# Cosine operands of an attention and expert kernel: the second batch scaled once, other ticks, own buffers for the first

## The chip, the cores and the metric

The kernel runs on one core of a Trainium2 chip. The metric is device time in microseconds (us), the median of several runs. One further execution was profiled; the rows below are from it.

## The reference

Three layers follow each other: attention with sink columns and a sliding window, a mixture of experts whose gate is balanced over rows and columns, and a two-layer network with the activation h cos(h).

```python
x = attention(q, k, v, n_sink=4, window=128)       # 2 batches of 768 rows, 512 wide
P = exp(x @ w_gate - max)                          # 8 experts
for _ in range(8):
    P /= P.sum(1); P /= P.sum(0); P *= N / E
y = sum(P[:, e:e+1] * (relu(x @ w1[e]) @ w2[e]) for e in range(8))   # 512 -> 1024 -> 512
h = y @ w_in                                       # 512 -> 2048
out = (h * cos(h)) @ w_out                         # 2048 -> 512
```

## The kernel before

All fp32 products are made from fp16 pairs: an operand is scaled by a power of two, its high half is the fp16 rounding, its low half the rest, and three matmuls (high x high, high x low, low x high) stand for one fp32 product. The products of the first matmul use a Winograd-like scheme: seven products of block sums instead of eight of blocks. So the left operand of a batch, `XO[b]`, holds seven blocks (two plain ones, four sums T, one plain one), each as a high and a low half, transposed.

The work runs as passes `layers(e, b)`: experts e = 0 to 7, and then the two halves of the 2048 columns of the cosine network, e = 8 and 9 (E = 8), each over both batches b. A pass has a first matmul (`g1` for experts, `g1_sums` for the cosine, 28 products of six matmuls of 128x384) and a second (`g2_mm`, 24 matmuls of 128x512 for each of six row tiles). In a cosine pass `g1_sums` goes through four columns j of seven products; part of the second matmul of three row tiles (`fill`) is put between the products, six such pieces are kept for the end (`KEEP`), and after the products come these six, then three for the last column but one (f = 3), then f = 7, then the three other row tiles whole. The hidden tile `hh` needs f = 3 and f = 7 of the first half of the batch at that point, and of the second half some microseconds later.

The order on the other engines is written by hand in ticks. `tick()` is called after each product of the first matmul (28 ticks, `GT`) and 24 times in the second (`HT_`); in a cosine pass the pieces after the products have one tick each up to the twelfth, and the other three row tiles four each. `put(t0, every, steps)` puts steps on coming ticks; `late` holds work for the next tick (`flush`). The engines take their instructions in that order but run ahead of or behind PE as their data allow.

The cosine (`act_cos`) of one 128x384 block goes ScalarE (L981, to an integer), VectorE (L984, the reduced angle), ScalarE (L989 sine, L990 square), VectorE (L993), GpSimd (L995 high half, L997 low half). L1094 is ScalarE's copy of the first product of a column, which frees a PSUM bank; L1086 is VectorE's sums of products.

An operand of the cosine network is made by `x_operand(b, c, i, s)` for six pairs (c, i) of a batch: T in three subtractions on POOL (L200 to L202), the high halves by ScalarE (L185), the low halves by VectorE as a scaled subtraction (L186, `x*s - hi`), and a transposing DMA from SyncE's queue (L208). Its result tile `xs` shares two buffers (tag `f64`) with the block sums S of the expert and cosine weights (`w1_split`, L310, on POOL); T has one buffer. `x2(b)` prepares the scale and the list of the six operands; `layers` puts them on ticks at the end of the first matmul of expert 7: for batch 0 into pass (7,1), every 7 ticks; for batch 1 three into the products of pass (8,0) and three into its second matmul. `XO[0]` is needed from the start of (8,0), `XO[1]` from the start of (8,1). `TMP` (13 tiles of 128x384 fp32) holds the scratch rings, such as `ring["c"]` for the products of an expert pass.

Of the kernel before, what the change touches and what calls it, by code (L numbers as in the profile page):

```python
# [10 lines left out]
F32 = mybir.dt.float32  # L11
F16 = mybir.dt.float16
# [3 lines left out]
AF = mybir.ActivationFunctionType  # L16
ALU = mybir.AluOpType
# [23 lines left out]
def kernel(  # L41
# [14 lines left out]
    nc = tc.nc  # L56
# [6 lines left out]
    E = w1.shape[0]  # L63
# [4 lines left out]
    U3 = NT // 2  # L68
# [3 lines left out]
    res = ctx.enter_context(tc.tile_pool(name="res", bufs=1))  # L72
    sm = ctx.enter_context(tc.tile_pool(name="sm", bufs=4))
    stage = ctx.enter_context(tc.tile_pool(name="stage", bufs=1))
# [4 lines left out]
    XO = [res.tile([128, 2, 7, 2, HT], F16, name=f"xo{b}") for b in range(B)]  # L79
# [42 lines left out]
    def scales(parts, n, clamp, keep, tag, then, squares=False, out=None, lag=2):  # L122

        p2 = sm.tile([128, n], F32, tag=f"p2{n}", name="p2")
        i = p2.bitcast(I32)
        nc.vector.tensor_scalar(out=p2, in0=parts, scalar1=clamp, scalar2=None, op0=ALU.max)
        if squares:  # L130

            nc.vector.tensor_scalar(
                out=i, in0=i, scalar1=0x7F800000, scalar2=1, op0=ALU.bitwise_and, op1=ALU.logical_shift_right)
            nc.vector.tensor_scalar(out=i, in0=i, scalar1=0x1FC00000, scalar2=None, op0=ALU.add)
        nc.vector.tensor_scalar(out=i, in0=i, scalar1=0x7F800000, scalar2=None, op0=ALU.bitwise_and)

        ds = [diag] if n == 1 else [W1O[:, NJ - 1, 1, k, 0].bitcast(BF16) for k in range(n)]
        for k, d in enumerate(ds):
            nc.scalar.activation(out=d, in_=eye, func=AF.Copy, scale=p2[:, k:k + 1])

        def product():
            bank = ring[top_bank[0]].next()
            held.append(bank)
            ps = bank[:, 0:n * 128].rearrange("p (n w) -> p n w", w=128)
            for k, d in enumerate(ds):
                nc.tensor.matmul(ps[:, k], one16, d, start=True, stop=True)
            late.append(lambda: rest(bank, ps))

        def rest(bank, ps):
            s, si = out or (keep.tile([128, n], F32, tag=f"{x}_{tag}", name="s") for x in ("s", "si"))  # L150
            nc.vector.tensor_reduce(out=si, in_=ps, axis=AX.X, op=ALU.max)
            held[:] = [h for h in held if h is not bank]
            nc.vector.reciprocal(out=s, in_=si)
            then(s, si)


        def after(n, f):
            late.append(f if n == 1 else lambda: after(n - 1, f))

        after(lag, product)  # L160

    def absmax(dst, src, axis=AX.X):
        nc.vector.tensor_reduce(out=dst, in_=src, axis=axis, op=ALU.max, apply_absolute_value=True)  # L163
# [9 lines left out]
        for f in now:  # L173
            f()

    def split(hi, lo, src, s=None, eng=None, by=0):

        if s is None:
            nc.scalar.activation(out=hi, in_=src, func=AF.Copy)
            late.append(lambda: (eng or nc.vector).tensor_tensor(out=lo, in0=src, in1=hi, op=ALU.subtract))  # L180
        else:
            if by:
                nc.vector.tensor_scalar(out=hi, in0=src, scalar1=s, scalar2=None, op0=ALU.mult)
            else:
                nc.scalar.activation(out=hi, in_=src, func=AF.Copy, scale=s)  # L185
            late.append(lambda: nc.vector.scalar_tensor_tensor(  # L186
                out=lo, in0=src, scalar=s, in1=hi, op0=ALU.mult, op1=ALU.subtract))

    def x_operand(b, c, i, s, place=None, g=nc.gpsimd, gl=nc.gpsimd):
# [21 lines left out]

        return rest


    def plain_operand(b, half, c, flat, gl):

# [39 lines left out]
    def w_load(e, nm, place, st, junk=None):  # L256

        n1 = 4 if nm == "w1" else NF
        n2 = FH if nm == "w1" else 512
        src = w_src(e, nm)  # L260

        def load(i):
            if i == 0:
                t = place if place is not None else stage.tile([128, 8, 512], F32, tag="st", name="st")
                st[nm] = t.rearrange("p a b -> p (a b)").rearrange("p (k f) -> p k f", k=n1)
                st[nm, "m"] = sm.tile([128, 4], F32, tag="wm", name="wm")
            i *= n1 // 4
            nc.sync.dma_start(out=st[nm][:, i:i + n1 // 4, :], in_=src[:, i:i + n1 // 4, :])

        def amax(i):  # L270
            n = n1 // 4
            dst, src = st[nm, "m"][:, i:i + 1], st[nm][:, i * n:(i + 1) * n, :].rearrange("p k f -> p (k f)")
            if junk is None:
                absmax(dst, src)
            else:
                squares(dst, src, junk)

        def scl():
            m = sm.tile([128, 1], F32, tag="wmm", name="wmm")
            nc.vector.tensor_reduce(out=m, in_=st[nm, "m"], axis=AX.X, op=ALU.max)  # L280
            scales(m, 1, 1e-30, res, f"{nm}{e}", lambda *s: wsc.update({(e, nm): s}), junk is not None, lag=2 if e else 5)

        return [lambda i=i: load(i) for i in range(4)] + [lambda i=i: amax(i) for i in range(4)] + [scl]

# [604 lines left out]
    def experts(before):  # L889
# [15 lines left out]
        def put(t0, every, steps):  # L905
            for n, f in enumerate(steps):
                at[int(now[0] + t0 + n * every)].append(f)
# [44 lines left out]
        def x2(b):  # L952

            a = ACC[b]
            m = sm.tile([128, NT], F32, tag="x2m", name="x2m")

            def scl():
                m1 = sm.tile([128, 1], F32, tag="x2n", name="x2n")
                nc.vector.tensor_reduce(out=m1, in_=m, axis=AX.X, op=ALU.max)
                scales(m1, 1, 1e-30, res, f"x2{b}", lambda *s: sx2.__setitem__(b, s))  # L960

            def ops(c, i):
                put(2, 1, [x_operand(b, c, i, sx2[b][0])])

            return ([lambda t=t: absmax(m[:, t:t + 1], a[:, t, :]) for t in range(NT)] + [scl],
                    [lambda c=c, i=i: ops(c, i) for c in range(2) for i in range(U3)])
# [178 lines left out]
        def layers(e, b, act, so):  # L1145

            fill = deque()
            ps = {}
            order = orders[e >= E]
            top_bank[0] = "l" if e < E else "g1"  # L1150
            if e == b == 0:
                for half in range(2):
                    g1_plain(b, half, act)
            elif e < E:
                for j0 in range(0, NJ, 2):
                    g1(b, j0, CHAIN, act)
            else:

                for j in range(NJ):
                    if j == 1:  # L1160
                        ps = {t: ring["g2"].next() for t in range(U3)}
                    for f in (j - 1, NJ + j - 1) if j else ():
                        for t in ps:
                            fill.append(lambda t=t, f=f: g2_mm(e, t, ps[t], [f], False))
                    g1_sums(b, j, act, fill, KEEP if j == NJ - 1 else 0)
            settle()
            if e < E:
                top_bank[0] = "C"
            if b == 0 and 1 <= e < E:
                if e == 1:  # L1170
                    ps_e(0)
                ps_e(e)
            if e == E - 1:
                amx, xops = x2(b)

                put(5, 4, [amx[t] for t in tiles])
                put(26, 1, amx[-1:])
                if b:

                    put(HT_ + 5, 7.0, xops[:3])  # L1180
                    put(HT_ + GT + 9, 4.0, xops[3:])
                else:
                    put(HT_ + 5, 7.0, xops)
            late = None
            if e >= E:
                for t in ps:
                    fill.append(lambda t=t: g2_mm(e, t, ps[t], order[-2:-1]))
                m = len(fill)
                for k in range(m):
                    fill.popleft()()  # L1190
                    for _ in range(U3 * (NJ - 1) * k // m, U3 * (NJ - 1) * (k + 1) // m):
                        tick()
                late = order[-1:]
            for t in tiles if 0 < e + b and e < E else range(NT):
                if t in ps:
                    g2_mm(e, t, ps[t], late)
                else:
                    ps[t] = ring["g2"].next()
                    g2_mm(e, t, ps[t], order)
                g2_out(e, b, t, ps[t], so)  # L1200
# [72 lines left out]
        for e in range(E + 2):  # L1273
# [35 lines left out]
            for b in range(B):  # L1309
                if b and not e:  # L1310
                    banks(A0=(2,), A1=(3,), B0=(6,), B1=(0,), C=(1,), l=(5,), x=(4,))
                    ring["c"] = Ring(TMP[:, n] for n in range(9))
                so = None
                act = act_relu
                if e >= E:
# [57 lines left out]
```

## Time and profile before

| | us |
|---|---|
| median of 3 runs | 1319.39 (1318.78 to 1319.42) |
| profiled execution, its own time | 1317.08 |
| its span, first to last instruction | 1315.3 |
| PE (TensorE matmul) busy | 1265.0, 96% |
| VectorE (DVE) busy | 856.5, 65% |
| ScalarE (ACT) busy | 697.7, 53% |
| GpSimd (POOL) busy | 635.3, 48% |
| mean granted clock of TensorE | 0.99 of full |

Busy time counts an engine's instructions without its waits. Shares over the whole span are means of stages with different limits; the passes around the change stand between about 1000 and 1195 us of the span.

### The profile page before, as it was taken

How to read it: one execution, taken by the hardware profiler on the slowest of the kernel's cores; microseconds unless marked ns; L12 is line 12 of the kernel's file. 1: busy time of each engine (PE TensorE's matmuls, PEld its weight loads, DVE VectorE, ACT ScalarE, POOL GpSimd, SP SyncE). 2: the span in 40 equal slices, each digit the busy share in tenths (PEclk: the TensorE clock that was granted, in tenths of full speed). 3: DMA queues.
4: the chain of work that ended last, by engine and by line, in shares of the span. 5: the costliest groups of instructions: out<-in, count | busy, mean ns of one | idle time of the engine just before them, and what ended most of it. 6: DMA issues, size and time to landing. Idle time of an engine off the chain costs nothing.

```text
span 1315.3 us, 19582 instructions
## 1 busy us (share of the span) xinstructions
PE 1265.0 (96%) x7275; PEld 668.7 (51%) x7275; DVE 856.5 (65%) x1671; ACT 697.7 (53%) x1399; POOL 635.3 (48%) x806
## 2 busy tenths in 40 slices
PE   5879999999999999999999999999999998999998
PEld 2545555545454555545455554545455444545454
DVE  6687866665657546654854665384466687878674
ACT  6877645536371644446163535526263667666462
POOL 5667625323441733274263437335342857376553
PEclk9799999999999999999999999999999998999999
DMA  9969640111115012310501231050121332400001
GB/s 270 213 149 214 102 117 1 65 65 65 35 53 185 1 65 87 122 65 12 198 1 64 80 129 44 22 183 26 65 70 57 57 92 29 106 1 1 36 14 49
DMA packets 130897, 105.50 MB, mean 80 GB/s; under 512 B 93296, under 2 KB 105840, under 8 KB 130800
## 3 DMA queue, kind: packets, MB, share of 16 engines
q1 hardware_dynamic: 118592, 75.51, 22.5%
q0 software_dynamic: 7168, 25.17, 6.0%
q10 hardware_dynamic: 5040, 3.56, 1.1%
q8 instruction: 57, 0.93, 0.3%
q14 instruction: 40, 0.33, 0.1%
HBM read 70.27 MB, written 11.53 MB: 62 GB/s over the span
## 4 chain that ended last, share of the span: by engine, by line
PE 72%; DVE 10%; POOL 6%; ACT 5%; issue 4%; DMA 3%; POOLq 0%; ACTq 0%; DVEq 0%
PE bank L1139 37%; PE bank L1055 29%; PE bank L1072 4%; POOL S L310 2%; DVE tmp L1086 1%; DMA parts<-parts 1%; DVE tmp L993 1%; DVE w1o L186 1%; DMA xo<-xs 1%; DMA parts<-xo 1%; DVE xo L596 1%; POOL hh L973 1%; PE bank L1122 1%; DVE w2s L186 1%; DVE tmp L984 1%
## 5 line engine op out<-in xcount | busy, mean ns | idle before, releaser
L1139 PE MATMUL bank<-w2s,hh 128*128 128x512 f16 x2880 | 637.3, 379 | 2.6 <-POOL hh L997 2.1
L1139 PEld LDWEIGHTS <-hh 128*128 128x128 f16 x2880 | 280.6, 98 | 334.3 <-POOL hh L997 4.8
L1055 PE MATMUL bank<-xo,w1o 128*128 128x384 f16 x2520 | 415.8, 327 | 0.6 <-ACT tmp L1023 0.6
L973 POOL TENSOR_TENSOR hh<-tmp,hh 128x384 f16<-128x384 f32 x240 | 218.0, 930 | 354.3 <-ACT tmp L972 352.4
L1055 PEld LDWEIGHTS <-w1o 128*128 128x128 f16 x2520 | 245.9, 98 | 164.4 <-issue 2.3
L1023 ACT ACTIVATE tmp<-bank 128x384 f32<-128x384 f32 x180 | 87.6, 488 | 298.5 <-PE bank L1055 298.4
L1027 DVE TENSOR_TENSOR tmp<-bank,tmp 128x384 f32<-128x384 f32 x180 | 97.7, 554 | 174.1 <-ACT tmp L1023 129.1
L1072 PE MATMUL bank<-xo,w1o 128*128 128x384 f16 x672 | 120.4, 329 | 6.9 <-ACT tmp L1094 3.7
L1211 DVE SCALAR_TENSOR_TENSOR acc<-bank,PS,acc 128x512 f32<-128x512 f32 x84 | 62.8, 748 | 81.6 <-PE bank L1139 81.2
L972 ACT ACTIVATE tmp<-tmp 128x384 f32<-128x384 f32 x180 | 94.1, 523 | 5.7
L1072 PEld LDWEIGHTS <-w1o 128*128 128x128 f16 x672 | 66.1, 99 | 58.3 <-issue 11.1
L971 ACT ACTIVATE hh<-tmp 128x384 f16<-128x384 f32 x180 | 92.6, 515 | 1.8 <-DVE tmp L1027 1.6
L995 POOL TENSOR_SCALAR hh<-tmp 128x384 f16<-128x384 f32 x64 | 45.9, 717 | 82.9 <-DVE tmp L993 73.1
L185 ACT ACTIVATE w1o<-S,s 128x1024 f16<-128x1024 f32 x37 | 42.4, 1145 | 74.5 <-POOL S L310 74.5
L163 DVE TENSOR_REDUCE wm<-st 128x1 f32<-128x1024 f32 x68 | 81.5, 1208 | 0.0
L310 POOL TENSOR_TENSOR S<-st 128x256 f32<-128x256 f32 x72 | 71.5, 993 | 16.5 <-DVE cr L862 9.2
L186 DVE SCALAR_TENSOR_TENSOR w1o<-st,s,w1o 128x512 f16<-128x512 f32 x72 | 65.1, 935 | 14.0 <-ACT w1o L185 13.9
L186 DVE SCALAR_TENSOR_TENSOR w2s<-st,s,w2s 128x512 f16<-128x512 f32 x72 | 60.1, 848 | 17.5 <-ACT w2s L185 17.4
L997 POOL TENSOR_TENSOR hh<-tmp,hh 128x384 f16<-128x384 f32 x64 | 68.8, 1075 | 5.3
L1086 DVE TENSOR_TENSOR tmp<-bank,tmp 128x384 f32<-128x384 f32 x112 | 59.1, 547 | 11.1 <-PE bank L1072 7.1
L186 DVE SCALAR_TENSOR_TENSOR w1o<-S,s,w1o 128x1024 f16<-128x1024 f32 x37 | 51.0, 1377 | 21.3 <-ACT w1o L185 21.3
L989 ACT ACTIVATE tmp<-tmp,scl 128x384 f32<-128x384 f32 x64 | 39.1, 610 | 26.9 <-DVE tmp L984 26.9
(193 smaller groups left out, 1310.7 us busy)
## 6 DMA issues: line engine op xcount, KB each, us to landing
st<-in_moe_w_dram SPq DMA_DIRECT2D x56, 512.0 KB, 6.0
f<-in_moe_w_in_dram POOLq DMA_DIRECT2D x16, 512.0 KB, 4.4
f<-in_moe_w_out_dram POOLq DMA_DIRECT2D x16, 512.0 KB, 4.2
w2p<-in_moe_w_dram SPq DMA_DIRECT2D x8, 512.0 KB, 4.1
w_in<-x POOLq DMA_DIRECT2D x16, 256.0 KB, 4.4
w_out<-x POOLq DMA_DIRECT2D x16, 256.0 KB, 4.2
st<-w_out SPq DMA_DIRECT2D x8, 512.0 KB, 5.5
st<-w_in SPq DMA_DIRECT2D x8, 512.0 KB, 6.4
```

Of the source, the lines that this page charges most:

```text
L163: nc.vector.tensor_reduce(out=dst, in_=src, axis=axis, op=ALU.max, apply_absolute_value=True)
L186: late.append(lambda: nc.vector.scalar_tensor_tensor(out=lo, in0=src, scalar=s, in1=hi, op0=ALU.mult, op1=ALU.subtract))
L310: g.tensor_tensor(out=q[:, n], in0=x, in1=y, op=op)
L971: nc.scalar.activation(out=hi, in_=src, func=AF.Relu)
L972: nc.scalar.activation(out=dst, in_=src, func=AF.Relu)
L973: nc.gpsimd.tensor_tensor(out=lo, in0=dst, in1=hi, op=ALU.subtract)
L1023: nc.scalar.activation(out=t, in_=ps, func=AF.Copy)
L1027: nc.vector.tensor_tensor(out=t, in0=ps, in1=t, op=ALU.add)
L1055: nc.tensor.matmul(ps, W1O[:, j0 + c, wi, o, kk, :], XO[b][:, kk, o, xi, :], start=(n == 0 and o in (0, 5, 1)), stop=(n == 5), skip_group_ ...
L1072: nc.tensor.matmul(ps, W1O[:, j, wi, o, kk, :], XO[b][:, kk, o, xi, :], start=(n == 0), stop=(n == 5))
L1086: nc.vector.tensor_tensor(out=t, in0=x, in1=y, op=ALU.add)
L1139: nc.tensor.matmul(ps, HH[:, t // U3, hi, f, (t % U3) * 128:(t % U3 + 1) * 128], w[:, wi, f, :], start=(f == order[0] and n == 0), stop=(f ...
```

## The change

Batch 1's x is scaled once in fp32 by VectorE into a tile X, and T and the low halves are then plain subtractions; T's low half goes to GpSimd. Batch 0's x is scaled in the low-half step as before; three of its six T go to VectorE, and its result tiles get two buffers of their own at the end of `TMP`, for which `ring["c"]` is cut to eight tiles in pass (7,1). Low halves come two ticks after their high halves (`lag=2`), not one, the transpose four ticks after T's high half, not two. The ticks change for both batches. The request for a scale of the last weights (`scales` in `w_load`, e = 9) waits five ticks, not two, for its diagonal product.

```diff
-            late.append(lambda: nc.vector.scalar_tensor_tensor(
+            after(lag, lambda: nc.vector.scalar_tensor_tensor(
                 out=lo, in0=src, scalar=s, in1=hi, op0=ALU.mult, op1=ALU.subtract))
...
+    def scaled_operand(b, c, i, s, xs, g):
+
+        x = ACC[b].rearrange("p (h t) (k w) -> p h t k w", h=2, w=128)[:, :, i, c::2]
+        T = stage.tile([128, 4, 128], F32, tag="z", name="T")
+        if b:
+            X = stage.tile([128, 2, 2, 128], F32, tag="x", name="X", bufs=2)
+            nc.vector.tensor_scalar(out=X, in0=x, scalar1=s, scalar2=None, op0=ALU.mult)
+            x = X
+        g.tensor_tensor(out=T[:, 1::2], in0=x[:, 1], in1=x[:, :, 0], op=ALU.subtract)
+        g.tensor_tensor(out=T[:, 2], in0=x[:, 1, 1], in1=T[:, 1], op=ALU.subtract)
+        g.tensor_tensor(out=T[:, 0], in0=x[:, 0, 1], in1=T[:, 2], op=ALU.subtract)
+
+        def part(src, o, gl):
+            hi, lo = xs[:, o, 0], xs[:, o, 1]
+            if b:
+                nc.scalar.activation(out=hi, in_=src, func=AF.Copy)
+                after(2, lambda: gl.tensor_tensor(out=lo, in0=src, in1=hi, op=ALU.subtract))
+            else:
+                split(hi, lo, src, s, lag=2)
+
+        part(x[:, 0], slice(0, 2), nc.vector)
+        part(x[:, 1, 1], 6, nc.vector)
+
+        def rest():
+            part(T, slice(2, 6), nc.gpsimd)
+            after(4, lambda: nc.sync.dma_start_transpose(
+                out=XO[b][:, c, :, :, i * 128:(i + 1) * 128].rearrange("p a l w -> p (a l) w"),
+                in_=xs.rearrange("p a l w -> p (a l w)")))
+
+        hooks[-1](2, 1, [rest])
...
-            scales(m, 1, 1e-30, res, f"{nm}{e}", lambda *s: wsc.update({(e, nm): s}), junk is not None, lag=2 if e else 5)
+            scales(m, 1, 1e-30, res, f"{nm}{e}", lambda *s: wsc.update({(e, nm): s}), junk is not None, lag=2 if 0 < e <= E else 5)
...
+            t = TMP.rearrange("p a b -> p (a b)")[:, -1792:].bitcast(F16).rearrange("p (n a l w) -> p n a l w", n=2, a=7, w=128)
+            own = Ring(t[:, n] for n in range(2))
+
             def ops(c, i):
-                put(2, 1, [x_operand(b, c, i, sx2[b][0])])
+                xs = stage.tile([128, 7, 2, 128], F16, tag="f64", name="xs", bufs=2) if b else own.next()
+                scaled_operand(b, c, i, sx2[b][0], xs, nc.gpsimd if b or U3 * c + i < 3 else nc.vector)
...
                 if b:
-                    put(HT_ + 5, 7.0, xops[:3])
-                    put(HT_ + GT + 9, 4.0, xops[3:])
+                    put(HT_ + 15, 5, xops)
                 else:
-                    put(HT_ + 5, 7.0, xops)
+                    put(HT_ + 5, 6, xops)
...
+                if b and e == E - 1:
+                    ring["c"] = Ring(TMP[:, n] for n in range(8))
```

## Rows read from the trace of the kernel before

**Rows 1.** The page, busy us, share of the span and instructions of each engine

```profile
PE 1265.0 (96%) x7275; PEld 668.7 (51%) x7275; DVE 856.5 (65%) x1671; ACT 697.7 (53%) x1399; POOL 635.3 (48%) x806
```

**Rows 2.** Timeline of PE: start us, us, instruction, matmuls, [idle before, releaser]

```profile
1062.27 0.65 PE L1072 MATMUL bank<-xo,w1o 128*128 128x384 f16 x3
...
1102.43 4.00 PE L1072 MATMUL bank<-xo,w1o 128*128 128x384 f16 x12 [3.20 <-ACT tmp L1094]
...
1130.61 0.65 PE L1072 MATMUL bank<-xo,w1o 128*128 128x384 f16 x3
...
1176.05 17.22 PE L1139 MATMUL bank<-w2s,hh 128*128 128x512 f16 x79 [0.38 <-POOL hh L997]
...
1252.64 10.89 PE L1072 MATMUL bank<-xo,w1o 128*128 128x384 f16 x66
...
1287.71 23.47 PE L1139 MATMUL bank<-w2s,hh 128*128 128x512 f16 x108
```

**Rows 3.** Waits of PE from 1002 to 1131: total us, times, longest

```profile
PE bank L1072 <- ACT tmp L1094: 3.2, 1, 3.2
PE bank L1072 <- DMA xo<-xs: 1.5, 1, 1.5
```

**Rows 4.** Waits of PE from 1130 to 1194

```profile
PE bank L1072 <- DMA xo<-xs: 1.3, 1, 1.3
...
PE bank L146 <- ACT diag L139: 0.7, 1, 0.7
```

**Rows 5.** One window: PE, PEld, DVE, ACT, POOL busy, granted clock, DMA

```profile
1097.40:1106.30 8.90, 5.31 (x21) 2.46 (x20) 6.50 (x14) 6.89 (x13) 5.72 (x6) 0.71 0.46 48
```

**Rows 6.** Waits of all engines from 1062 to 1131

```profile
DVE xs L186 <- ACT xs L185: 11.3, 9, 3.9
...
POOL hh L995 <- DVE tmp L993: 8.5, 6, 2.9
```

**Rows 7.** Line 180, a plain low half, on DVE: instructions, count, shortest/median/longest ns

```profile
L180 DVE TENSOR_TENSOR tmp<-acc,tmp x12: 281/349/418, 154.4 to 170.1; 128x256 f16<-128x256 f32 x6, 128x128 f16<-128x128 f32 x6
```

**Rows 8.** Timeline of SyncE's queue, the last transpose of batch 0

```profile
1060.34 1.53 SPq L208 DMA_TRANSPOSE xo<-xs  x1
```

**Rows 9.** Tile xs (columns as rows 7)

```profile
L186 DVE SCALAR_TENSOR_TENSOR xs<-acc,s,xs x24: 341/770/997, 1009.1 to 1125.4; 128x256 f16<-128x256 f32 x12, 128x128 f16<-128x128 f32 x12
...
L186 DVE SCALAR_TENSOR_TENSOR xs<-T,s,xs x12: 735/750/1502, 1011.9 to 1127.5; 128x512 f16<-128x512 f32 x12
...
DMA to landing us min/median/max: 3.9/4.0/5.3
```

**Rows 10.** Timeline of POOL, last subtraction of the first chain in (7,1)

```profile
1021.08 0.92 POOL L973 TENSOR_TENSOR hh<-tmp,hh 128x384 f16<-128x384 f32 x1 [0.43 <-ACT tmp L972]
```

**Rows 11.** Timeline of ACT, first copies of the second chain in (7,1)

```profile
1020.91 0.85 ACT L1023 ACTIVATE tmp<-bank 128x384 f32<-128x384 f32 x2
```

**Rows 12.** Groups of DVE by line and form: busy us, mean ns, idle before

```profile
L1209 DVE TENSOR_SCALAR acc<-acc,PS 128x512 f32<-128x512 f32 x12 | 6.2, 517 | 0.0
```

**Rows 13.** Tile T on POOL, whole trace (columns as rows 7)

```profile
L200 POOL TENSOR_TENSOR T<-acc x12: 723/755/1633, 993.5 to 1124.5; 128x256 f32<-128x256 f32 x12
L201 POOL TENSOR_TENSOR T<-acc,T x12: 455/458/901, 994.3 to 1125.3; 128x128 f32<-128x128 f32 x12
L202 POOL TENSOR_TENSOR T<-acc,T x12: 455/460/653, 994.8 to 1125.9; 128x128 f32<-128x128 f32 x12
L180 POOL TENSOR_TENSOR tmp<-T,tmp x6: 1156/1161/1617, 155.2 to 170.7; 128x512 f16<-128x512 f32 x6
```

**Rows 14.** Tile hh on POOL from 1062 to 1131 (columns as rows 7)

```profile
L995 POOL TENSOR_SCALAR hh<-tmp x16: 508/740/817, 1073.1 to 1115.1; 128x384 f16<-128x384 f32 x16
L997 POOL TENSOR_TENSOR hh<-tmp,hh x16: 912/1172/1317, 1073.9 to 1115.7; 128x384 f16<-128x384 f32 x16
```

**Rows 15.** Timeline of POOL, finishers in (8,0) and (8,1)

```profile
1112.20 1.09 POOL L997 TENSOR_TENSOR hh<-tmp,hh 128x384 f16<-128x384 f32 x1
...
1151.37 0.82 POOL L995 TENSOR_SCALAR hh<-tmp 128x384 f16<-128x384 f32 x1 [2.36 <-DVE tmp L993]
```

More of the change, by code (lines that the diff above doesn't have):

```diff
@@ L154, in rest, with after @@
             then(s, si)
-        def after(n, f):
-            late.append(f if n == 1 else lambda: after(n - 1, f))
         after(lag, product)
+    def after(n, f):
+        late.append(f if n == 1 else lambda: after(n - 1, f))
     def absmax(dst, src, axis=AX.X):
@@ L174, in flush, with split @@
             f()
-    def split(hi, lo, src, s=None, eng=None, by=0):
+    def split(hi, lo, src, s=None, eng=None, by=0, lag=1):
         if s is None:
```

## The prediction

> **What bounds the kernel now.** I read the busy shares first. TensorE (PE) is busy for 1265.0 of 1315.3 us [rows 1], so only a wait of PE, or a stretch in which its clock falls, can be won. The PE timeline then shows where there are such stretches. Call a pass over one batch of an expert or cosine half (half, batch): (7,1), (8,0), (8,1), and so on. The last pass, (9,1), has no waits: its products start at 1252.64, its second matmul at 1287.71, so 35.1 us, and its 108 second matmuls take 23.5; together 58.5 [rows 2]. Pass (8,0) runs from 1062.27 to 1130.61 [rows 2], 68.3 us, and so loses 9.8. This is the pass in which batch 1's operands are formed, and at whose start batch 0's must be ready.
>
> The waits of PE name the losses: 3.2 us for ScalarE's copy of a product (L1094) and 1.5 for the transposed operands of batch 0 [rows 3]; at the start of (8,1) 1.3 for those of batch 1, and later 0.7 for a diagonal [rows 4]. Right behind the 3.2 us twelve matmuls take 4.00 us, where 66 take 10.89 in (9,1) and twelve thus 2.0 [rows 2]; the granted clock of that stretch is 0.71 [rows 5], a mixture of 2.4 and 1.2 GHz. That is 2 us more.
>
> Why was L1094 late? ScalarE (ACT) and VectorE (DVE) hand the cosine to each other in program order, and DVE stood 11.3 us in nine waits until ACT had formed an operand's high half, with the cosine's steps queued behind it. POOL waited 8.5 us for DVE's L993 [rows 6]: it was the engine with time left.
>
> **Batch 0's operands in (7,1).** Six operands come every 6 ticks instead of 7, the last at tick 35, not 40; its transpose is issued two ticks later after its start than before, so 3 ticks sooner in all. It weighs more that its blocks leave the buffers shared with the weight sums S, so that POOL's S no longer waits for transposes and T no longer stands behind S. Three of the six T move to DVE: one subtraction of 128x256 and two of 128x128, 0.42 and twice 0.28 us by the ends of L180 there [rows 7], 1 us each. The last transpose was issued at 1060.34 [rows 8] and lands 4.0 us later [rows 9]. The bounds are 0 and the 1.5 us that PE waited; three ticks of that second matmul, six matmuls of 0.217 us each, are 3.9 us, so I take all 1.5. If DVE's queue, which has to cover the three T, is that late, the wait comes back.
>
> The ring of scratch tiles for the expert products shrinks to eight, which is just what one chain of 14 products takes. The second tile of the next chain is still read by POOL's last subtraction (to 1021.08 + 0.92 [rows 10]) when ACT's copy wants it (1020.91 [rows 11]): 1.1 us late, or nothing if POOL gets there earlier. I charge 0.6.
>
> **Batch 1's operands in (8,0).** They stood at ticks 5, 12, 19 of the products and 9, 13, 17 of the second matmul; now at 15, 20, 25 and at 2, 7, 12. For each:
> - DVE makes one scaling of 128x512, 0.52 us by L1209 [rows 12], and plain subtractions of 0.42 and 0.28 [rows 7], instead of three scaled ones, twice 0.77 and 0.75 [rows 9]: 1.2 us, not 2.3. It no longer waits for the high half of T, and for the others it comes a tick later.
> - ACT makes the same three copies.
> - POOL makes T as before, 0.76 + 0.46 + 0.46 = 1.67 us, and one more subtraction of 128x512, 1.16 by L180 [rows 13].
>
> Of three operands ahead of L1094 in the last column, one and the first part of another remain there. So I take the 3.2 us and the slow clock behind them as gone; the bounds are nothing left and 3 us left.
>
> **What is late next is POOL.** A finisher of the cosine (L995, L997) takes 0.74 + 1.17 = 1.91 us [rows 14] and is put 4 ticks after its product. From tick 13 to 27 POOL's queue holds nine of them, and now three T (ticks 15, 20, 25) and two low halves (19, 24). In (8,1) the finisher of tick 13 began at 1151.37 [rows 15], 19.4 us after the pass ran freely (1130.61 [rows 2] and the wait of 1.3 [rows 4]); I take 20.0, because in (8,0) squares are on ACT too. Then the low half of column 3, first half of the batch, is ready 20.0 + 9 x 1.91 + 3 x 1.67 + 2 x 1.16 = 44.5 us after the pass begins. PE wants it at 35.1 + 20 matmuls of 0.217, at 39.4. So I expect PE to wait some 5 us in one piece. Column 7 follows a low half and a finisher later, at 47.6. The clock will probably fall again behind that wait; the few matmuls before column 7 hide this but for 0.8 us. From there 79 matmuls take 17.2 us, as from 1176.05 on in (8,1) [rows 2], so that the pass ends at 65.6. Today column 7's low half ended at 1112.20 + 1.09 [rows 15], 51.0 us after 1062.27, and the pass ended at 68.3. So (8,0) wins 2.7 of its 9.8 us, the 1.5 at its start among them.
>
> The bounds: with all these rows at their shortest (1.42, 1.63, 1.16 [rows 13, 14]) column 3 comes at 40.0; at their longest (2.13, 3.19, 1.62) at 52.0. I take the medians, because DVE is as busy beside them as before.
>
> The Trainium skill, SBUF — State Buffer, section "Who interferes with whom", says that a VectorE instruction with two SBUF inputs, or a tensor_scalar in a two-port mode, and a GpSimd instruction that reads SBUF shut each other out of a shared pair of ports. The spread of L995 (508 to 817 ns) and of L997 (912 to 1317) [rows 14] agrees with it. By this rule each scaling pass could hold POOL for its whole length, three of them 1.6 us before column 3, and column 3 would come at 46.1.
>
> **The last operand.** After column 7 POOL makes T, two finishers and a low half (54.3). The transpose lands 4.0 us later [rows 9] and frees a block for the sixth operand's high half; copies and its own low half are some 3.4 us, another 4.0 us of transfer gives 65.7, or 68 with the longest landing of 5.3 [rows 9]. PE wants it at 66.2, after three matmuls of (8,1). Today that was 1130.61 + 0.65 + 1.3, at 70.3. I take 67.2, so up to here 3.1 us are won.
>
> The diagonal's product comes 5 ticks after its request, not 2, and the 0.7 us of (8,1) [rows 4] go.
>
> **Sum.** -3.1 - 0.7 + 0.6 = -3.2 us on the profiled execution, which took 1317.08 (span 1315.3). The median shown, 1319.39, lies 2.3 above it; I put the difference on the median: 1316.2.
>
> **Rivals.**
> - *POOL is held back* (longest rows): column 3 at 52.0, column 7 at 55.8, the pass ends at 73.0 to 73.8, and batch 1's start is 74.0 to 74.5, up to 4.2 us later than today; with -0.7 and +0.6 that is 1323.4. For it: every step given to POOL meets DVE at its busiest, and ACT's copy of T then waits for POOL with the cosine behind it. Against it: DVE has fewer instructions with two inputs. It decides from the point where column 7 is ready later than 51 us after the pass begins. The page's rule is a reason for this case.
> - *POOL in between*, finishers at their longest alone: column 3 at 46.5, column 7 at 49.8, end near 67.8, restart at 69: 1.3 us won, 1318.0, no change that shows.
> - *POOL is not the bound* (shortest rows): column 7 at 42.6, or near 44.6 when POOL still waits for DVE's L993 for a quarter of today's 8.5 us [rows 6]. The pass ends near 62, the last operand lands at 62.5: 7.8 us won, 1311.5. For it: DVE's waits for ACT mostly go. Against it: the medians.
> - *The edit doesn't act* on batch 0: ticks order the queues only, and its last transpose could stay late behind DVE. Then 1.5 of the gain is lost, 1317.7; this lies within the cases above.
>
> **How the numbers follow.** 0.2% is 2.6 us, about what a measurement of this kernel can tell from no change. The forecast has 0.35 (its own range is 1314 to 1318), in between and the unmoved batch 0 together 0.34, POOL held back 0.19, POOL not the bound 0.12. So faster 0.47, same 0.34, slower 0.19. The range goes from the last rival's 1311.5 to 1322.5, just short of the longest rows, which can hardly all come together.
>
> **What would show it.** In the changed profile: no wait for xo<-xs before (8,0), and none of 3 us for L1094; instead a wait of L1139 for POOL's L997 of 4 to 7 us early in the second matmul of (8,0), with a granted clock under 1 behind it; POOL busy some 7 us more in this pass; no wait for the diagonal in (8,1). If the L1139 wait is under 2 us, or (8,1) starts with a wait of over 3 us, or (7,1) is over 1.5 us longer, that step is wrong.

## The result: slower, 1328.6 us against 1319.8

The changed kernel takes 1328.59 us (median of 8 runs, 1327.3 to 1333.6), the kernel before 1319.78 in the same session (8 runs). The ratio is 1.0066 [1.0042, 1.0091]. The forecast was 1316.2, so the sign is wrong too, and the time lies above the range. The profiled execution of after took 1327.3, with a span of 1325.6; the span of before is 10.3 shorter.

First, where the 10.3 us are. On the PE timeline a pass runs from its first product to the next pass's first product:

| us | start of (7,1) | (7,1) | (8,0) | (8,1) | (9,0) |
|---|---|---|---|---|---|
| before | 1002.80 | 59.47 | 68.34 | 62.50 | 59.53 |
| after | 1000.74 | 64.75 | 77.11 | 60.74 | 59.52 |
| difference | -2.06 | +5.28 | +8.77 | -1.76 | 0.0 |

So the growth lies in (7,1) and (8,0), the two passes in which operands are formed. (7,1) starts 2.1 us sooner and (8,1) is 1.8 shorter. The page's busy times hardly move [rows 1]:

```profile
PE 1264.4 (95%) x7275; PEld 667.7 (50%) x7275; DVE 867.2 (65%) x1680; ACT 695.7 (52%) x1399; POOL 635.9 (48%) x803
```

The PE timeline of after answers to [rows 2, 3] (start, us, engine, line, operation, tiles; in brackets the idle time ahead and its releaser). Old L1094 is now L1129, L1139 is L1174, L995 and L997 are L1030 and L1032, L1023 is L1058, L1213 is L1248.

```profile
1019.42 1.14 PE L1090 MATMUL bank<-xo,w1o 128*128 128x384 f16 x6 [1.84 <-ACT tmp L1058]
1021.90 12.67 PE L1090 MATMUL bank<-xo,w1o 128*128 128x384 f16 x60 [1.34 <-ACT tmp L1058]
...
1065.49 5.04 PE L1107 MATMUL bank<-xo,w1o 128*128 128x384 f16 x30
...
1100.03 2.11 PE L1107 MATMUL bank<-xo,w1o 128*128 128x384 f16 x12 [1.20 <-ACT tmp L1129]
...
1106.95 0.22 PE L146 MATMUL bank<-diag,one 128*128 128x128 bf16 x1 [2.22 <-ACT diag L139]
...
1109.52 0.60 PE L1174 MATMUL bank<-w2s,hh 128*128 128x512 f16 x2 [1.06 <-POOL hh L1030]
1110.92 1.68 PE L1174 MATMUL bank<-w2s,hh 128*128 128x512 f16 x7 [0.79 <-POOL hh L1032]
1113.13 0.60 PE L1174 MATMUL bank<-w2s,hh 128*128 128x512 f16 x2 [0.53 <-POOL hh L1030]
1114.18 1.68 PE L1174 MATMUL bank<-w2s,hh 128*128 128x512 f16 x7 [0.44 <-POOL hh L1032]
1124.27 18.49 PE L1174 MATMUL bank<-w2s,hh 128*128 128x512 f16 x72 [8.41 <-ACT acc L1248]
1142.60 10.89 PE L1107 MATMUL bank<-xo,w1o 128*128 128x384 f16 x66
...
1175.92 3.08 PE L1107 MATMUL bank<-xo,w1o 128*128 128x384 f16 x18 [0.96 <-ACT tmp L1129]
```

Up to 1115.9 the pass (8,0) goes nearly as forecast. Then comes a wait that no step of the forecast holds: 8.41 us for L1248, ScalarE's eviction of the first three row tiles, which frees the PSUM banks that the other three need. The 72 matmuls behind it take 18.49 us, where the same 72 take 15.70 in e2 and e6 below: 2.8 us of slow clock. The windows of the wait and of the stretch behind it have granted clocks of 0.64 and 0.63 (columns as in [rows 5]: window, PE, PEld, DVE, ACT, POOL busy, clock, DMA share, GB/s):

```profile
1118.00:1124.30 6.30, 0.03 (x1) 0.02 (x1) 2.11 (x3) 1.34 (x4) 5.24 (x8) 0.64 0.35 65
1124.30:1132.00 7.70, 7.70 (x23) 2.87 (x23) 3.86 (x5) 4.05 (x8) 3.75 (x5) 0.63 0.57 109
```

Why was an eviction late whose inputs PE had finished? ACT's timeline shows what stood ahead of it:

```profile
1017.30 0.72 ACT L185 ACTIVATE tmp<-T,s 128x512 f16<-128x512 f32 x1 [1.88 <-POOL T L225]
...
1021.36 0.49 ACT L1058 ACTIVATE tmp<-bank 128x384 f32<-128x384 f32 x1 [1.02 <-POOL hh L1008]
...
1113.82 0.60 ACT L230 ACTIVATE xs<-X 128x256 f16<-128x256 f32 x2
1116.65 0.63 ACT L230 ACTIVATE xs<-T 128x512 f16<-128x512 f32 x1 [2.23 <-POOL T L225]
1117.45 0.61 ACT L230 ACTIVATE xs<-X 128x256 f16<-128x256 f32 x2 [0.17 <-DVE X L221]
1123.02 0.63 ACT L230 ACTIVATE xs<-T 128x512 f16<-128x512 f32 x1 [4.96 <-POOL T L225]
1123.55 1.83 ACT L1248 ACTIVATE acc<-bank,scl 128x512 f32<-128x512 f32 x3
```

The first two rows are from (7,1) and are read with e4 and e5 below. In (8,0) the three evictions stand behind the copies of the fourth and the fifth operand's T. ACT idles 2.23 and 4.96 us in front of these, with the evictions queued behind. POOL, which makes T, is not idle meanwhile:

```profile
1109.55 1.31 POOL L1032 TENSOR_TENSOR hh<-tmp,hh 128x384 f16<-128x384 f32 x1
...
1113.16 0.96 POOL L1032 TENSOR_TENSOR hh<-tmp,hh 128x384 f16<-128x384 f32 x1
...
1118.91 0.91 POOL L1032 TENSOR_TENSOR hh<-tmp,hh 128x384 f16<-128x384 f32 x1
1119.78 1.33 POOL L231 TENSOR_TENSOR xs<-T,xs 128x512 f16<-128x512 f32 x1
1121.19 0.72 POOL L223 TENSOR_TENSOR T<-X 128x256 f32<-128x256 f32 x1
1122.00 0.46 POOL L224 TENSOR_TENSOR T<-X,T 128x128 f32<-128x128 f32 x1
1122.53 0.46 POOL L225 TENSOR_TENSOR T<-X,T 128x128 f32<-128x128 f32 x1
```

Ahead of the fifth T stand finishers of the cosine and the fourth operand's low half (L231), which reads the T whose only buffer the fifth needs. So one operand passes DVE (X), POOL (T), ACT (high half) and POOL (low half) before the next T can be made, and PE's banks hang on the ACT link of that chain. These rows show no pause of POOL for the buffer: its own queue holds the fifth T up here.

### The profile page after: what moved, and what is told of

Read it like the earlier page. It is cut to its first block, busy times and chain, and to the rows that moved or that the text cites. A ratio compares the mean times of both kernels' runs of the same rounds, so it can differ in the third digit from the quotient of the medians.

```text
span 1325.6 us, 19597 instructions
## 1 busy us (share of the span) xinstructions
PE 1264.4 (95%) x7275; PEld 667.7 (50%) x7275; DVE 867.2 (65%) x1680; ACT 695.7 (52%) x1399; POOL 635.9 (48%) x803
## 4 chain that ended last, share of the span: by engine, by line
PE 76%; DVE 9%; ACT 5%; POOL 4%; issue 4%; DMA 2%; ACTq 0%; SPq 0%; POOLq 0%; DVEq 0%
PE bank L1174 40%; PE bank L1090 29%; PE bank L1107 4%; DVE tmp L1121 2%; PE bank L1157 1%; POOL S L341 1%; DMA parts<-parts 1%; PE bank L617 1%; DVE tmp L1028 1%; ACT xo L637 1%; DVE xo L627 1%; DVE w1o L186 1%; DVE w2s L186 1%; POOL hh L1032 1%; DVE tmp L1019 1%
## 5 line engine op out<-in xcount | busy, mean ns | idle before, releaser
L1174 PE MATMUL bank<-w2s,hh 128*128 128x512 f16 x2880 | 639.8, 380 | 12.6 <-ACT acc L1248 8.4
L1174 PEld LDWEIGHTS <-hh 128*128 128x128 f16 x2880 | 281.2, 98 | 347.7 <-issue 15.5
L1058 ACT ACTIVATE tmp<-bank 128x384 f32<-128x384 f32 x180 | 87.7, 488 | 302.1 <-PE bank L1090 301.0
L1030 POOL TENSOR_SCALAR hh<-tmp 128x384 f16<-128x384 f32 x64 | 45.7, 714 | 92.1 <-DVE tmp L1028 91.5
L1032 POOL TENSOR_TENSOR hh<-tmp,hh 128x384 f16<-128x384 f32 x64 | 67.3, 1052 | 5.3
```

Source lines behind the costliest of these rows:

```text
L1058: nc.scalar.activation(out=t, in_=ps, func=AF.Copy)
L1174: nc.tensor.matmul(ps, HH[:, t // U3, hi, f, (t % U3) * 128:(t % U3 + 1) * 128], w[:, wi, f, :], start=(f == order[0] and n == 0), stop=(f ...
```

## The experiments

For (8,0) the theories are: **A**, the order in ACT's queue (evictions behind copies that wait for T); **B**, POOL has too much to do (its new low halves). For (7,1) the question is which part of batch 0's edit costs the time: the ring of eight or the spacing of six ticks. Unless said otherwise the diff is against the changed kernel. The table has what was measured, the passes as above, from one profiled execution each. A ratio goes by the runs of the kernel before in the same session (medians 1319.88 to 1320.46). Runs of one kernel spread over some 10 us, so where there is one run only the passes are read:

| label | (7,1) | (8,0) | (8,1) | time, us | ratio to before |
|---|---|---|---|---|---|
| e1_two_late | 61.98 | 69.63 | 60.75 | 1320.49 | 1.0003 [0.9984, 1.0022] |
| e2_old_ticks | 61.99 | 65.11 | 63.39 | 1321.3 | 1.0000 [0.9975, 1.0026] |
| e3_lo_vector | 61.99 | 75.89 | 60.74 | 1327.8 | one run |
| e4_shared_ring13 | 60.83 | 77.03 | 60.73 | 1328.29 | one run |
| e5_ring10 | 60.86 | 77.19 | 60.75 | 1327.31 | one run |
| e6_evict_vector | 63.27 | 69.72 | 60.73 | 1321.56 | one run |
| e7_old_ticks_ring13 | 59.69 | 67.24 | 63.38 | 1322.24 | 1.0006 [0.9985, 1.0026] |
| e8_four_two | 59.69 | 67.70 | 60.74 | 1315.95 | 0.9967 [0.9945, 0.9988] |
| e9_own_ring10 | 59.68 | 67.37 | 60.72 | 1317.77 | 0.9996 [0.9973, 1.0019] |
| e10_old_operand | 59.45 | 75.40 | 61.01 | 1328.09 | 1.0057 [1.0034, 1.0080] |
| e11_early_four | 59.68 | 67.34 | 60.72 | 1317.4 | 0.9974 [0.9951, 0.9996] |
| e12_lag2 | 59.68 | 67.38 | 61.02 | 1322.68 | one run |

**e1: two operands behind the evictions.**

```diff
-                    put(HT_ + 15, 5, xops)
+                    put(HT_ + 15, 5, xops[:4])
+                    put(HT_ + 40, 4, xops[4:])
```

> The changed kernel with batch 1's fifth and sixth operand at ticks 40 and 44 instead of 35 and 40, behind the evictions of the first three row tiles of (8,0); nothing else. Theory A (the 8.4 us wait of PE is ACT's queue: the evictions L1248 stand behind the high half of the fifth operand's T, which waits for POOL): that wait and the slow clock behind it go, (8,0) falls from 77.1 us to 66 to 69; the sixth operand then lands late and (8,1) may begin with a wait of 1 to 4 us; the time falls by 5 to 9 us against the changed kernel, to 1320 to 1323. Theory B (POOL's added work alone sets the pass, whatever is queued on ACT): (8,0) stays over 74 us, and the wait turns up at hh or at the operands.

Its PE timeline, where the evictions are waited for:

```profile
1116.88 17.39 PE L1174 MATMUL bank<-w2s,hh 128*128 128x512 f16 x72 [2.05 <-ACT acc L1249]
```

On ACT's timeline:

```profile
1115.62 0.63 ACT L230 ACTIVATE xs<-T 128x512 f16<-128x512 f32 x1 [2.23 <-POOL T L225]
1116.16 1.83 ACT L1249 ACTIVATE acc<-bank,scl 128x512 f32<-128x512 f32 x3
```

The wait shrinks from 8.41 to 2.05 and (8,0) by 7.5 us, to just above the 66 to 69 expected. All else of the change is still there, POOL's steps too. What is left stands behind the fourth T, still ahead of the evictions.

**e2: the ticks of before with the new operand.**

```diff
-                    put(HT_ + 15, 5, xops)
+                    put(HT_ + 5, 7, xops[:3])
+                    put(HT_ + GT + 9, 4, xops[3:])
```

> The changed kernel with batch 1's six operands at the ticks of the kernel before (5, 12, 19 and, in the second matmul, 9, 13, 17); operand, low halves on GpSimd and delays as changed. Theory A (the place in ACT's queue makes the loss): no wait for L1248 over 1 us, (8,0) at 66 to 69 us with some wait for L1129 left, time 1320 to 1323. Theory B (POOL's added work): (8,0) at 73 us or more.

```profile
1101.73 2.11 PE L1107 MATMUL bank<-xo,w1o 128*128 128x384 f16 x12 [1.52 <-ACT tmp L1129]
...
1115.21 15.70 PE L1174 MATMUL bank<-w2s,hh 128*128 128x512 f16 x72 [0.73 <-ACT acc L1249]
1133.88 10.40 PE L1107 MATMUL bank<-xo,w1o 128*128 128x384 f16 x63 [2.49 <-DMA xo<-xs]
```

(8,0) takes 65.1 us, 12.0 less than in after and under the 66 to 69 expected, and the 72 matmuls run at full speed. In exchange the operands are late for (8,1), which waits 2.49 us for them and grows by 2.6.

**e3: T's low halves from POOL to VectorE (theory B's price).**

```diff
-            part(T, slice(2, 6), nc.gpsimd)
+            part(T, slice(2, 6), nc.vector)
```

> The changed kernel with the low half of T of batch 1 on VectorE instead of GpSimd; all ticks as changed. Theory A (ACT's queue: evictions behind the high half of the fifth operand's T, which waits for POOL's T): POOL reaches that T some 5 us sooner (four low halves of 1.34 us fewer before it), so the wait for L1248 falls from 8.4 us to 3 to 5, and (8,0) from 77.1 to 70 to 74 us. Theory B (POOL's load is the whole cause): (8,0) falls to the 68 us of before or under it.

(8,0) wins only 1.2 us, less than either theory gave it. The PE timeline, and POOL's around the fifth T:

```profile
1109.19 0.22 PE L146 MATMUL bank<-diag,one 128*128 128x128 bf16 x1 [3.10 <-ACT diag L139]
...
1124.70 18.58 PE L1174 MATMUL bank<-w2s,hh 128*128 128x512 f16 x72 [5.78 <-ACT acc L1248]
```

```profile
1120.53 0.96 POOL L1032 TENSOR_TENSOR hh<-tmp,hh 128x384 f16<-128x384 f32 x1
1121.45 0.90 POOL L223 TENSOR_TENSOR T<-X 128x256 f32<-128x256 f32 x1
```

Here (8,0) begins at 1005.24 + 61.99 = 1067.23. The fifth T starts 54.2 us after that, in after 1121.19 - 1065.49 = 55.7: the low half ahead of it is gone, no more. The finisher in front ends at the same time in both, 54.3 us after the start of the pass. So with the low halves gone from POOL, T comes 1.5 us sooner, and (8,0) wins 1.2 of the 8.8 us. B falls as the main cause; T still comes long after ACT reaches its copy. What VectorE's added work costs in this run isn't separated from that.

**e6: the three evictions on VectorE.**

```diff
+            elif e == E and b == 0 and t < U3:
+                nc.vector.tensor_scalar(out=a, in0=ps, scalar1=so, scalar2=None, op0=ALU.mult)
```

> The changed kernel with the evictions of the first three row tiles of (8,0) on VectorE instead of ScalarE; operands, ticks and POOL's work untouched. Theory A: the wait for the eviction falls from 8.4 us to 2 to 4 us (VectorE has the fifth operand's low half ahead of it), and (8,0) to 67 to 72 us. Theory B (POOL's load): (8,0) stays at 75 to 77, the wait only takes another name.

```profile
1121.35 15.70 PE L1174 MATMUL bank<-w2s,hh 128*128 128x512 f16 x72 [3.24 <-DVE acc L1248]
```

With ticks, T, X and POOL's work untouched, (8,0) falls by 7.4 of the 8.8 us: taking the evictions out of ACT's queue is enough for that. PE waits 3.24 us for them in DVE's queue instead. Both of theory A's figures (2 to 4, and 67 to 72) hold.

**e10: the kernel before with the new ticks alone** (old operand, scaled three times; diff against before).

```diff
-                    put(HT_ + 5, 7.0, xops[:3])
-                    put(HT_ + GT + 9, 4.0, xops[3:])
+                    put(HT_ + 15, 5, xops)
```

> The kernel before, whole, with one edit: batch 1's six operands at the new ticks (15 to 40 every 5). The old operand has a scaled low half on VectorE with a delay of one tick. Theory A (the place in ACT's queue): an eviction wait L1214 of 4 us or more appears here too, (8,0) grows from 68.3 to 73 to 78 us, and the time by 5 to 10 us. Theory B (the new operand's work on GpSimd makes the loss): (8,0) stays within 2 us of 68.3.

```profile
1110.16 0.27 PE L146 MATMUL bank<-diag,one 128*128 128x128 bf16 x1 [4.33 <-ACT diag L139]
...
1125.65 17.64 PE L1139 MATMUL bank<-w2s,hh 128*128 128x512 f16 x72 [5.31 <-ACT acc L1213]
```

```profile
1124.31 0.72 ACT L185 ACTIVATE xs<-T,s 128x512 f16<-128x512 f32 x1 [3.81 <-POOL T L202]
1124.93 1.82 ACT L1213 ACTIVATE acc<-bank,scl 128x512 f32<-128x512 f32 x3
```

The same picture without X and without a low half on POOL: ACT waits 3.81 us for T, the evictions stand behind it, and (8,0) takes 75.4 us, as theory A had it. So the move of the ticks alone makes 7.1 of the 8.8 us by which (8,0) grew. Its ratio, 1.0057, overlaps that of the whole change.

**e4 and e5: a longer ring for the products of (7,1).** e4 shares the old buffers and gives the ring all 13 tiles; e5 keeps the own buffers and adds two spare tiles.

```diff
-                xs = stage.tile([128, 7, 2, 128], F16, tag="f64", name="xs", bufs=2) if b else own.next()
+                xs = stage.tile([128, 7, 2, 128], F16, tag="f64", name="xs", bufs=2)
...
-                    ring["c"] = Ring(TMP[:, n] for n in range(8))
+                    ring["c"] = Ring(TMP[:, n] for n in range(13))
```

> The changed kernel with batch 0's result tiles back in the buffers shared with the weight sums, and the scratch ring of (7,1) back at thirteen tiles; every tick as changed. Theory C (the ring of eight makes the loss of (7,1)): the 1.34 us wait for L1058 that follows POOL's hh goes, the 1.84 us wait that follows POOL's T stays or halves, (7,1) falls from 64.8 us to 60 to 62. Theory D (the spacing of six, which puts the high half of T ahead of the copies): (7,1) stays above 63 us. By both the last operand of batch 0 may be late at (8,0) by up to 1.5 us.

```diff
-                    ring["c"] = Ring(TMP[:, n] for n in range(8))
+                    ring["c"] = Ring([TMP[:, n] for n in range(8)] + [
+                        stage.tile([128, 512], F32, tag="x", name="spare", bufs=2)[:, 0:HT] for _ in range(2)])
```

> The changed kernel with two more scratch tiles in the ring of (7,1), ten instead of eight, from buffers that are idle there; batch 0's result tiles stay in their own buffers. Theory C (the ring of eight): as with thirteen tiles, (7,1) at 60 to 62 us and the time 2.5 to 4.5 us below the changed kernel's. Theory D (spacing): (7,1) above 63 us.

In both (7,1) is 60.8 us and (8,0) as in after. In after's ACT timeline stand the two causes, of which e4's PE timeline shows only the second: L1058 waits for POOL's last subtraction (the ring; this wait is gone with 10 or 13 tiles), and ahead of it a copy of T waits for POOL (the spacing; this is left, and PE still waits 1.8 us for it):

```profile
1024.44 1.14 PE L1090 MATMUL bank<-xo,w1o 128*128 128x384 f16 x6 [1.81 <-ACT tmp L1058]
```

The time, expected 2.5 to 4.5 us below after's, is 1327.31 in the one run of e5, within after's runs; only the pass shows the gain. The own buffers themselves bring nothing that these runs show: (8,0) takes 77.03 us with shared and 77.19 with own ones, and in both PE no longer waits for batch 0's operands.

**e7: ticks of before for batch 1, nearly so for batch 0, long ring.** As e2 and e4, and for batch 0:

```diff
-                    put(HT_ + 5, 6, xops)
+                    put(HT_ + 5, 7, xops[:2])
+                    put(HT_ + 18, 6, xops[2:])
```

> Both losses undone together: batch 1's operands at the ticks of before, batch 0's tiles in the shared buffers with a scratch ring of thirteen, and batch 0's ticks at 5, 12, 18, 24, 30, 36, so that the second operand's T stands on ACT where it stood before. Theory D (the spacing of six puts that T ahead of a copy that PE wants): the 1.84 us wait for L1058 falls to 0.5, (7,1) to 59.5 us; with (8,0) at 65 and (8,1) at 63.4 as measured with the old ticks, the time is 2 to 4 us below the kernel before, 1316 to 1318. If the spacing is not the cause, the wait stays at 1.8 us and (7,1) at 60.8.

(7,1) comes to 59.7: with the second operand at tick 12, not 11, the last wait there shrinks to 0.66 us. But (8,0) takes 67.24 us, not the 65 expected from e2:

```profile
1109.90 3.33 PE L1107 MATMUL bank<-xo,w1o 128*128 128x384 f16 x12 [2.60 <-ACT tmp L1129]
```

PE now waits longer for L1129 than in e2 (2.60 against 1.52 us), and the twelve matmuls behind it take 3.33 instead of 2.11. (7,1) and (8,0) together take 126.9 us here and 127.1 in e2: what (7,1) wins, (8,0) loses again. Why L1129 doesn't come sooner with it stays open; e9 rules out the shared buffers. The time, expected at 1316 to 1318, is 1322.24. The three passes take 190.31 us together, as in before: with operands at about the old ticks, the new ones win nothing that shows.

**e8: e4, batch 0 as in e7, and four operands of batch 1 early, two behind the evictions.**

```diff
-                    put(HT_ + 15, 5, xops)
+                    put(HT_ + 5, 6, xops[:4])
+                    put(HT_ + 40, 4, xops[4:])
```

> As the run before, but batch 1's operands at ticks 5, 11, 17, 23 of the products and 40, 44 behind the evictions, so that no copy of T stands ahead of an eviction and the last transpose is issued one tick sooner. Theory A: no wait for L1248 over 0.5 us; the wait of (8,1) for the last operand falls from 2.5 us to 0 to 2; (8,0) 64 to 67 us, and the time 3 to 6 us below the kernel before. Theory B (POOL's load): four operands within the products bring POOL's waits for hh to 3 to 5 us, and the time is no lower than with the old ticks.

```profile
1099.89 3.79 PE L1107 MATMUL bank<-xo,w1o 128*128 128x384 f16 x12 [2.49 <-ACT tmp L1129]
...
1112.83 17.22 PE L1174 MATMUL bank<-w2s,hh 128*128 128x512 f16 x79 [0.37 <-POOL hh L1032]
```

No wait for an eviction is left, and (8,1) has none for operands; the copy L1129 is late again, 2.49 us with a slow clock behind, as it was in before [rows 3]. The three passes take 188.1 us, 2.2 less than before, and the ratio is 0.9967 [0.9945, 0.9988]: 0.3% below the kernel before, with an interval that just leaves 1 out. (8,0), at 67.70, is longer than the 64 to 67 expected.

**e9: e8 with own buffers and e5's ring.**

> The four-and-two version with batch 0's result tiles in their own buffers again and the ring at ten tiles with two tiles that are idle elsewhere. Theory F (the shared buffers delay the weight sums at the end of (7,1) and with them VectorE's evictions and the cosine's start): (7,1) stays near 59.7 us, the first cosine step of (8,0) comes some 0.7 us sooner, the wait for L1129 falls from 2.5 to 1 to 2 us, (8,0) from 67.7 to 65 to 66.5, and the time is 4 to 6 us below the kernel before. If the buffers don't matter at (8,0), it stays at 67.5 and the time at 0.997 of the kernel before.

(8,0) is 67.37 us against e8's 67.70, and the wait for L1129 is 2.58 us against 2.49: theory F falls. The ratio is 0.9996; its interval and e8's overlap, and the two are not told apart.

**e11: e9 with the early four at ticks 5, 9, 13, 17** (diff against e9).

```diff
-                    put(HT_ + 5, 6, xops[:4])
+                    put(HT_ + 5, 4, xops[:4])
```

> As the run with ten tiles, but the first four operands of batch 1 at ticks 5, 9, 13, 17 instead of 5, 11, 17, 23. If ACT's work ahead of the last column's L1129 sets its wait, all four stand ahead of it now and the wait grows by 1 to 2 us, (8,0) by 1 to 3 us; if idle time of the first columns takes them up, (8,0) is 0 to 1.5 us shorter.

Neither expectation describes it. The PE timeline shows a wait at another place, for POOL's hh in the midst of the products; L1129's falls to 1.12, and (8,0) stays at 67.34:

```profile
1090.19 1.65 PE L1174 MATMUL bank<-w2s,hh 128*128 128x512 f16 x3 [3.39 <-POOL hh L1030]
...
1104.73 2.11 PE L1107 MATMUL bank<-xo,w1o 128*128 128x384 f16 x12 [1.12 <-ACT tmp L1129]
```

**e12: e9 with the diagonal's old lag** (diff against e9).

```diff
-            scales(m, 1, 1e-30, res, f"{nm}{e}", lambda *s: wsc.update({(e, nm): s}), junk is not None, lag=2 if 0 < e <= E else 5)
+            scales(m, 1, 1e-30, res, f"{nm}{e}", lambda *s: wsc.update({(e, nm): s}), junk is not None, lag=2 if e else 5)
```

> As the run with ten tiles, but the diagonal of the last weights 2 ticks after its request, as in the kernel before. By the prediction's term (8,1) has a wait of 0.7 us for the diagonal back and is 0.4 to 0.7 us longer. The rival: the wait for the diagonal only changes places with one for L1129 (0.95 us in all runs with five ticks), and (8,1) stays within 0.3 us of 60.74; in (8,0) the diagonal is asked for 2 us sooner by PE and the wait there grows.

(8,1) takes 61.02 us, against 60.72 in e9. The longer lag is worth 0.3 us there, not 0.7: with it the 0.67 for the diagonal goes and 0.94 for L1129 comes. In (8,0) the wait for the diagonal is 2.39 us with the old lag and 0.20 in e9, as the rival had it, but the pass is the same (67.38 and 67.37): in e9 waits for hh stand in its place. The first line is e12's, the others are e9's:

```profile
1114.32 0.22 PE L146 MATMUL bank<-diag,one 128*128 128x128 bf16 x1 [2.39 <-ACT diag L139]
...
1110.55 0.61 PE L1174 MATMUL bank<-w2s,hh 128*128 128x512 f16 x2 [0.97 <-POOL hh L1030]
1111.95 2.12 PE L1174 MATMUL bank<-w2s,hh 128*128 128x512 f16 x9 [0.79 <-POOL hh L1032]
```

## Why the prediction was wrong

**The step that failed** is the end of (8,0): "From there 79 matmuls take 17.2 us". The forecast followed POOL into `hh` and stopped there. It counted the banks as free, because in [rows 2] they were, with three of the operands in the second matmul at other ticks. In the changed order only 7 matmuls ran from there, and then PE waited 8.41 us and lost 2.8 by the clock. The text said that ACT's copy of T would wait for POOL "with the cosine behind it", but not that evictions stand in the same queue. e1, e6 and e10 show it from three sides: the ticks alone make the wait, and moving either the operands or the evictions takes most of it away. The rival "POOL is held back" had the right sign, by another mechanism: it let hh come late, past 51 us after the pass began, and hh was ready at 48.6.

**The POOL step was right in its times, not in its wait.** Column 3's low half was forecast 44.5 us after the pass began and came at 1110.86 - 1065.49 = 45.4 (from 1109.55 + 1.31 on POOL); that of column 7 at 1113.16 + 0.96 - 1065.49 = 48.6, forecast 47.6. POOL's busy time in the pass rose from 39.75 to 47.74 us, 8.0; forecast 7. But the hit is in part luck. The first of the nine finishers began 17.3 us after the start of the pass, not 20.0, and what POOL did from there on took 28.1 us instead of 24.5: the three T alone 7.2 us from start to next start, not 5.0, and POOL idled another 2.0 for DVE.

```profile
1082.76 0.74 POOL L1030 TENSOR_SCALAR hh<-tmp 128x384 f16<-128x384 f32 x1 [0.65 <-DVE tmp L1028]
```

PE's waits up to there are 2.22 + 1.06 + 0.79 + 0.53 + 0.44 = 5.0 us, forecast "some 5 us in one piece". By the forecast's own sign, a wait for L997 (now L1032) under 2 us, the step is wrong: those for L1032 are 0.79 and 0.44. The first and largest is for the diagonal; the waits of e9 and e12 show that the one for the diagonal and those for hh stand in for each other.

**Batch 0's wait of 1.5 us** before (8,0) [rows 3] is gone, as forecast, but not for the reason that was said to weigh more, the own buffers: in e4, with shared ones, it is gone too. (8,1) no longer waits for operands (-1.76 with the diagonal). L1129's 3.2 us fell to 1.20, not to nothing.

**"I charge 0.6" for (7,1)** was too little. The waits of 1.84 and 1.34 make the pass 2.5 us longer (61.98 in e1 to e3, with 59.47 in before), and in the profiled execution of after the clock fell behind them, 2.8 more. Half of the waits is the ring, as named (1.1 us less in e4 and e5, the upper of the two values that the forecast had), the other half the copy of T that the spacing of six ticks puts ahead of L1058 (e4, e5, e7): no step held that. The forecast's sign for this, (7,1) longer by over 1.5 us, came.

**"1.2 us, not 2.3" for DVE per operand** was too low, as were the "1 us each" for batch 0's T on DVE in (7,1) (medians of 0.95, 0.89 and 0.70 us for its three steps, together 2.5). The tiles X and xs in after (min/median/max ns, first to last start):

```profile
L221 DVE TENSOR_SCALAR X<-acc,s x6: 668/932/1455, 1084.0 to 1118.9; 128x512 f32<-128x512 f32 x6
L231 DVE TENSOR_TENSOR xs<-X,xs x12: 415/566/999, 1088.0 to 1126.4; 128x256 f16<-128x256 f32 x6, 128x128 f16<-128x128 f32 x6
L231 POOL TENSOR_TENSOR xs<-T,xs x6: 1153/1336/1482, 1092.9 to 1127.8; 128x512 f16<-128x512 f32 x6
```

0.93 + 2 x 0.57 is 2.1 us, hardly less than the old three. In e2 the same scaling has a median of 0.48 us, though its longest takes 1.22 too:

```profile
L221 DVE TENSOR_SCALAR X<-acc,s x6: 468/480/1220, 1071.7 to 1124.8; 128x512 f32<-128x512 f32 x6
```

In after the last one took 1.22 us, on DVE's timeline from 1118.89 on, beside L1032 and L231 on POOL (above):

```profile
1118.89 1.22 DVE L221 TENSOR_SCALAR X<-acc,s 128x512 f32<-128x512 f32 x1
```

The rule on shared ports (the Trainium skill, SBUF — State Buffer, "Who interferes with whom") would make a scaling in a two-port mode longer beside such steps of POOL. These rows agree, though not every such overlap lengthens a scaling: in e2 the one at 1093.65 took 0.47 us with POOL busy during 0.40 of them. Which mode the scaling ran in no row shows. The low halves on POOL cost 1.34 us, not the 1.16 of L180.

**The diagonal**, -0.7, was 0.3 (e12).

The forecast's net gain of 3.2 us thus had its gains (batch 0's wait, (8,1)'s start) and POOL's delay about right, the latter in part by luck, and left out 11.2 us in (8,0) and, at least, 1.9 in (7,1). Whether T would come sooner ahead of the finishers in POOL's queue, or with a second buffer, wasn't tried.

## What to carry to other kernels

When a step moves in an order written by hand, list for each in-order queue what stands behind every instruction of it that can wait, evictions of PSUM banks first: the step's own deadline says nothing about them. A chain that passes several engines with one buffer stops each of their queues in turn; keep it out of the ticks just before an eviction, as e8, e9 and e11 do (188.1, 187.8 and 187.7 us for the three passes, 190.3 before). And charge a wait of PE of some microseconds with a slow clock behind it: here 1.7 us more behind 2.05 (e1) and 2.8 behind 8.41 (after), but nothing behind 3.24 (e6).

## What the hardware did unexpectedly

The clock did not fall behind the same waits each time: after 1.84 and 1.34 us of waiting in (7,1) 60 matmuls took 12.67 us in after's profile, 11.20 in e6's and 9.91 in e1's, at the same place of the same code up to there. So 2.8 us of after's span are not in every execution, nor are 1.3 of e6's (7,1). The start of (7,1) also differed, from 1000.7 to 1012.5 us over the executions; time before it says nothing about the edits, which is why the passes are compared here and the ratios rest on repeated runs.
